# A third tile for the pre-mix's input in a talking-heads attention and MoE kernel

## The chip, the cores and the metric

The kernel runs on one core of one Trainium2 chip. The metric is device time in microseconds (us) of one execution, as the median of several runs; lower is better. TensorE multiplies matrices, VectorE (DVE) and ScalarE (ACT) work on elements, GpSimd (POOL) does a few elementwise steps, and SyncE (SP) issues DMAs. ScalarE and GpSimd can issue DMAs too.

## What is computed

Attention with 4 batches, 12 heads, 448 tokens and 64 dimensions, in which the scores of the 12 heads are mixed before the softmax (`w_pre`) and after it (`w_post`); then two feed-forward layers on the 1792 tokens.

```python
def _attn_ref(q, k, v, w_pre, w_post):
    scores = scale * np.matmul(q, k.transpose(0, 1, 3, 2))
    scores = np.einsum('bhij,hg->bgij', scores, w_pre)
    ...softmax over j...
    attn = np.einsum('bhij,hg->bgij', attn, w_post)
    return np.matmul(attn, v)
...
x = attn_out as (1792, 768)
x = elu(x @ moe_w_in) @ moe_w_out                     # 768 -> 2048 -> 768
x = layer_norm(solu(x @ moe2_w_in)) * g_ln @ moe2_w_out   # 768 -> 1024 -> 768
```

## The kernel before

**Chunks.** The attention runs over 17 chunks of query rows (`CH`), numbered 0 to 16. A chunk holds 4 to 12 groups of ten query rows of one batch. Chunks 0 to 4 belong to batch 0, 5 to 8 to batch 1, 9 to 12 to batch 2, 13 to 16 to batch 3.

**Scores and moves.** For each pair of heads of a chunk there is one score step on TensorE (`mm` in `add_score`, L443), which fills two PSUM banks. VectorE or ScalarE copies each bank to an SBUF buffer `sev` (`evac`, L449; 8 buffers, `SB`). A DMA, called a move here (`move`, issued at L400), then carries the rows of that head to their place in the chunk's tile `sp`, in which 12 heads of a group of query rows lie on neighbouring partitions. The last head takes two moves, so a chunk has 13. A `sev` buffer is free again when its move has landed.

**Pre-mix, softmax, post-mix.** Two groups make a unit; there are 90. A unit's pre-mix (`pre`, L510) multiplies the rows of `sp` with `wpre_t`. It needs all moves of the chunks that it reads, so the first unit of a chunk waits for the chunk's last move. VectorE finds the maximum (L515), ScalarE the exponential (L520), GpSimd the weights of the post-mix (L531), and TensorE does the post-mix (`post`, L543), whose result is copied to `at` (L551). When a chunk's units are through, TensorE multiplies `at` with the values (L592), and the result goes by way of `x` (L599) to `xs` in device memory.

**Two tiles.** `sp` has two tiles, in the pools `spa` and `spb`, that chunks use in turn: chunk c writes the tile of chunk c-2 (L453, L463). They are cleared once (L470), the first by VectorE, the other by GpSimd. The keys lie in a pool `k` of 12 tiles (L130); a batch needs six.

**What sets the order.** All steps of the attention are given to `op` with a rank (a planned time), what they depend on, the buffers that they take or use, and a cost on each engine that may do them. `schedule` (L296) then picks, again and again, the step that can start first and, on that engine, the one with the lowest rank, and emits it. So each engine's order is fixed when the program is built. The ranks of a chunk's scores are spread between the planned pre-mix start of the chunk ahead of it and `SCM` us ahead of its own (L391 to L393). With `lag` a step's result counts as there so many us after its planned end; moves have 3.5. The moves of chunks 0 and 1 may go by SP or ScalarE, those of chunk 2 by SP or GpSimd, all others by SP (L461).

**DMA completion.** The DMAs that SP and ScalarE issue share eight completion semaphores (`DMAHW0` to `DMAHW7` in the rows of order) by turns: each waits until the eighth before it in the program has landed. Those that GpSimd issues have others (`DMASW`).

After the attention, `start_moe` (L662) releases the pools on the right side of the memory and starts the loads of the first feed-forward layer.

Of the kernel before, what the change touches and what calls it, by code (L numbers as in the profile page):

```python
# [9 lines left out]
F32 = mybir.dt.float32  # L10
# [8 lines left out]
NB, NH, S, D = 4, 12, 448, 64  # L19
# [5 lines left out]
NC = len(CH)  # L25
# [12 lines left out]
XB = 2  # L38
# [12 lines left out]
DB = .9  # L51
DA = .2
T0 = 14
SCM = 12
KD = 3.5
VD = 28
WB = 3
SB = 8
VB = 2
EB = 10  # L60
LEAD = 3

@with_exitstack
def kernel(ctx: ExitStack, tc: tile.TileContext, qa, kt, vt, wpre, wpost,
# [6 lines left out]
    pools = {}  # L71

    def pool(name, bufs=1, side="left", space=None):
        kw = {"space": space} if space is not None else {"side": side}
        p = tc.alloc_tile_pool(name=name, bufs=bufs, reuse_waits="tile", **kw)
        pools[name] = p
        return p

    def release(*names):
        for n in names:  # L80
            pools.pop(n).release()
# [45 lines left out]
    wpost_t = const.tile([128, 60], F32, name="wpost_t")  # L127

    pool("spa", 1, "right")
    k_p = pool("k", 12, "right")  # L130
    kst_p = pool("kst", 2, "right")
    q_p = pool("q", 4, "right")
    sev_p = pool("sev", SB, "right")
# [72 lines left out]
    def w1_alloc(fg, p):  # L206
        w1[fg] = tuple(p.tile([128, 1536], F32R, tag=t, name=t) for t in ("wih", "wil", "woh", "wol"))
# [6 lines left out]
    def xT_alloc(tb, p):  # L214
        xT[tb] = (p.tile([128, ECH, S], F32R, name=f"xh{tb}"), p.tile([128, ECH, S], F32R, name=f"xl{tb}"))
# [63 lines left out]
    class Op:  # L279
# [2 lines left out]
    ops = []  # L282
    tail = {"pe": .3, "act": .2, "dve": .17, "pool": .1, "sp": 2.0, "host": 0.0}
    bufs = {"sc": 3, "pm": 3, "po": 2, "sev": SB, "e": EB, "wr": WB, "st": 4, "kst": 2, "q": 4,
            "k": 12, "sp0": 1, "sp1": 1, "at": 2, "v": VB, "x": XB, "ws": 4, "wy": 2}

    def op(rank, emit, deps=(), new=(), uses=(), more=0.0, lag=None, **us):

        o = Op()
        o.rank, o.emit, o.deps, o.new, o.us, o.more, o.lag = rank, emit, [d for d in deps if d is not None], new, us, more, lag  # L290
        for b in chain(new, uses):
            b.users.append(o)
        ops.append(o)
        return o
# [61 lines left out]
    def copier(e):  # L356
        return nc.scalar.copy if e == "act" else nc.vector.tensor_copy
# [6 lines left out]
    def plan_front():  # L364
        nonlocal t, nf
        if nf < NU:
            t_pre[nf] = t
            c = units[nf][1][0]
            t += PRE + (6 * SC / (first[c + 1] - first[c]) if c + 1 < NC else 0.0)
            nf += 1  # L370

    pending = []
    for u in range(NU):
        while nf < min(NU, u + LEAD + 1):
            plan_front()
# [14 lines left out]
    for c in range(NC):  # L390
        lo, hi = (t_pre[first[c - 1]], t_pre[first[c]] - SCM) if c > 1 else (T0 - 5, T0 - 1) if c else (2, T0 - 6)  # L391
        for h in range(0, NH, 2):
            t_sc[c, h] = lo + (h + 1) * (hi - lo) / NH  # L393

    kt_t, kb, q_t, qb_, sp_t, sp_op, pre_op, e_t = {}, {}, {}, {}, {}, {}, {}, {}
# [3 lines left out]
    def dma(out, in_, e="sp"):  # L399
        {"act": nc.scalar, "pool": nc.gpsimd, "sp": nc.sync}[e].dma_start(out=out, in_=in_)  # L400
# [27 lines left out]
    def add_score(c, h):  # L428

        b, _, G = CH[c]  # L430
        n = 5 * G
        ring = ("sc", "pm")[h // 2 % 2] if c == 0 else "sc"
        scb, svb = [Buf(ring) for _ in range(2)], [Buf("sev") for _ in range(2)]
        r = t_sc[c, h]
        key = "sc", c, h

        def mm(e):
            T[key] = [pools["ps_" + ring].tile([128, 512], F32, tag=ring, name="sc") for _ in range(2)]
            q, k = q_t[c, h // 6], kt_t[b, h]
            for x in range(2):  # L440
                for i in range(2):
                    sl = slice(64 * i, 64 * i + 64)
                    nc.tensor.matmul(T[key][i][64 * x:64 * x + 64, :S], q[sl, h % 6 // 2, 64 * x:64 * x + 64], k[sl, :],  # L443
                                     start=True, stop=True)

        def evac(e, i):
            t = T["sv", c, h + i] = (k0.tile([128, S], F32, name=f"s0_{h + i}") if c == 0 else
                                     sev_p.tile([128, S], F32, tag="sev", name="sev"))
            copier(e)(t, T[key][i][:, :S])  # L449

        def move(e, i, p, r0, r1):
            if c not in sp_t:
                sp_t[c] = sp_t[c - 2]  # L453
            dma(sp_t[c][p:p + 13 * (r1 - r0 - 1) + 1:13, 0:G, :], T["sv", c, h + i][r0 * G:r1 * G], e)

        o1 = op(r, mm, [k_op[b, h], q_op[c, h // 6]], scb, [qb_[c, h // 6], kb[b, h]], pe=SC)
        for i in range(2):
            sv = [] if c == 0 else [svb[i]]
            o2 = sc_ev[c, h + i] = op(r + .9 + .1 * i, lambda e, i=i: evac(e, i), [o1], sv, [scb[i]], act=.43, dve=.54)
            for n, to in enumerate([(h + i, 0, 10)] if h + i < 11 else [(11, 0, 5), (64, 5, 10)]):  # L460
                sp_op.setdefault(c, []).append(op(r + 2 + .2 * i + .1 * n, lambda e, i=i, to=to: move(e, i, *to), [o2], [spb_[c]], sv, lag=3.5, sp=.78, **({"act": .78} if c < 2 else {"pool": 1.0} if c == 2 else {})))  # L461

    spb_ = {c: Buf(f"sp{(NC - c) % 2}") for c in range(NC)}  # L463
    o = op(7.0, lambda e: dma(wpre_t, wpre), sp=.5)
    o_wpost = op(T0 + 2, lambda e: dma(wpost_t, wpost), sp=.5)
    w_op = op(T0 - 8, lambda e: nc.gpsimd.tensor_scalar(wpre_t, wpre_t, 0.125, None, ALU.mult), [o], pool=.6)

    for c in range(2):
        sp_t[c] = pools["spb" if (NC - c) % 2 else "spa"].tile([128, NH, S], F32, tag="sp", name="sp")
        (nc.gpsimd if c else nc.vector).memset(sp_t[c], 0.0)  # L470
    for t in po_p:
        nc.vector.memset(t, 0.0)
# [1 line left out]
    def begin(e):  # L474
        release("k0")
        pool("at", 2)
        pool("e", EB)
        pool("wr", WB)
# [4 lines left out]
    for c in range(NC):  # L483
        b = CH[c][0]
        if c == HEAD[b]:
            for h in range(0, NH, 2):
                add_k(b, h)
        for hf in range(2):
            add_q(c, hf)
        for h in range(0, NH, 2):  # L490
            add_score(c, h)
# [78 lines left out]
    for c in range(NC):  # L570
# [12 lines left out]
        for n in range(2):  # L583
            r = t_av[c, n]
# [76 lines left out]

    def start_moe(e):  # L662
        nonlocal gln_t
        release("sev", "q", "kst", "k", "spa")
        p = pool("wstg", 2, "right")
        gln_t = p.tile([128, F2 // 128], F32, name="gln_t", bufs=1)
        dma(gln_t, gln)
        w1_alloc(0, pool("w1a", 1, "right"))
        xT_alloc(0, pool("xT0", 1, "right"))

    gln_t = None
    lc = NC - 1
    t0 = t_pre[first[lc]]
    o_moe = op(t0, start_moe, sp_op[lc] + [pre_op[last_of[lc - 1]], T["ws", 15]] +
               [k_op[NB - 1, NH - 2]], host=0.0)
    need = []
# [41 lines left out]
    for i in range(3):  # L718
        ws = Buf("ws")
# [252 lines left out]
```

## Time and profile before

| | us |
|---|---|
| median of 3 runs | 1096.0 (1095.16 to 1097.95) |
| the profiled execution, its own time | 1094.9 |
| its span, first to last instruction | 1093.1 |
| TensorE busy in the span | 1059.9 (97%) |
| VectorE / ScalarE / GpSimd busy | 722.0 / 504.2 / 231.6 |

The attention takes the first 370 us or so; the first feed-forward layer runs up to about 840 us, the second to the end. In the list of the costliest groups the score, pre-mix and post-mix matmuls have 123.8, 112.2 and 109.1 us. A matmul's end is modelled, so two that follow closely are shown to overlap, and a short wait between them is not shown as idle time. A float32 matmul of the program stands as two records in the trace: a unit's pre-mix has four matmuls and eight records.

### The profile page before, as it was taken

What the parts mean: (1) busy time and instruction counts of PE and PEld (TensorE: products, weight loads), DVE (VectorE), ACT (ScalarE), POOL (GpSimd) and SP (SyncE); (2) the same over time, 40 slices, a digit from 0 to 9 for tenths busy, and PEclk for the clock granted to TensorE, in tenths of its full rate; (3) what the DMA queues carried; (4) which work ended last, traced back from release to release, by engine and by line L of the source; (5) the groups of instructions that cost most, each with busy time, mean ns of one, the idle gap of its engine ahead of it and who ended that gap; (6) DMA issues with size and microseconds to landing.
All of it is one profiled execution on the core that took longest, in us unless ns stands there. A gap on an engine that the chain in (4) does not pass through costs nothing.

```text
span 1093.1 us, 28427 instructions
## 1 busy us (share of the span) xinstructions
PE 1059.9 (97%) x11800; PEld 888.6 (81%) x11800; DVE 722.0 (66%) x1391; ACT 504.2 (46%) x1071; POOL 231.6 (21%) x243
## 2 busy tenths in 40 slices
PE   6899999999999999999999999999999999999998
PEld 2457667667666898998988999999999889898988
DVE  6576687677677557687887887878864644353522
ACT  3566676677676455333333443333431434342422
POOL 2211010011011325343343433343431000000000
PEclk9999999999999999999999999999999999999999
DMA  6875775775746442415234242423262400000001
GB/s 200 210 209 172 216 238 172 219 221 176 232 149 197 132 133 72 155 58 171 99 117 149 83 154 77 140 91 126 70 243 100 194 30 15 30 23 22 30 15 44
DMA packets 80287, 141.69 MB, mean 130 GB/s; under 512 B 20853, under 2 KB 59969, under 8 KB 80157
## 3 DMA queue, kind: packets, MB, share of 16 engines
q1 hardware_dynamic: 78345, 136.59, 39.1%
q10 hardware_dynamic: 1332, 2.09, 0.6%
q8 instruction: 93, 1.52, 0.6%
q0 software_dynamic: 480, 1.19, 0.4%
q14 instruction: 37, 0.30, 0.1%
HBM read 75.96 MB, written 25.17 MB: 93 GB/s over the span
## 4 chain that ended last, share of the span: by engine, by line
PE 74%; DMA 9%; DVE 8%; ACT 4%; issue 2%; SPq 1%; POOL 1%; ACTq 0%; DVEq 0%; POOLq 0%
PE h L256 15%; PE o L745 15%; PE o L888 11%; PE h L841 11%; PE av L592 6%; PE sc L443 5%; PE pm L510 5%; PE po L543 5%; DMA sp<-sev 3%; DMA ws<-in_wo_dram 2%; DVE x L761 1%; DVE wy L184 1%; DMA ws<-in_wi_dram 1%; PE tr L872 1%; DVE wq L180 1%
## 5 line engine op out<-in xcount | busy, mean ns | idle before, releaser
L520 ACT ACTIVATE e<-pm,st 128x448 f32<-128x448 f32 x180 | 113.4, 635 | 72.3 <-DVE st L515 65.9
L515 DVE TENSOR_REDUCE st<-pm 128x1 f32<-128x448 f32 x180 | 105.1, 617 | 60.9 <-PE pm L510 58.6
L745 PE MATMUL o<-gh,woh 128*128 128x448 f32 x384 | 141.3, 368 | 3.8 <-ACT x L759 1.9
L745 PE MATMUL o<-glo,woh 128*128 128x448 f32 x384 | 139.9, 364 | 0.0
L745 PE MATMUL o<-gh,wol 128*128 128x448 f32 x384 | 139.8, 364 | 0.0
L443 PE MATMUL sc<-kt,q 64*64 64x448 f32 x816 | 123.8, 565 | 9.7 <-ACT sev L449 4.6
L543 PEld LDWEIGHTS po<-wr,e 60*64 60x64 f32 x5040 | 102.4, 135 | 37.0 <-issue 23.8
L269 POOL TENSOR_TENSOR glo<-g,gh 128x448 fp32r<-128x448 f32 x64 | 83.1, 1298 | 217.9 <-issue 124.5
L510 PE MATMUL pm<-sp,wpre_t 64*64 64x448 f32 x720 | 112.2, 558 | 10.4 <-DMA xs<-x 4.4
L888 PE MATMUL o<-w,lh 128*128 128x384 f32 x448 | 120.3, 340 | 0.0
L543 PE MATMUL po<-wr,e 60*64 60x60 f32 x5040 | 109.1, 219 | 2.3 <-issue 1.1
L841 PE MATMUL h<-w,x2h 128*128 128x512 f32 x336 | 107.7, 395 | 0.0
L761 DVE TENSOR_TENSOR x<-x,o 128x448 f32<-128x448 f32 x168 | 101.4, 610 | 7.9 <-PE o L745 7.9
L256 PE MATMUL h<-xh,wih 128*128 128x448 f32 x288 | 105.5, 366 | 0.0
L256 PE MATMUL h<-xh,wil 128*128 128x448 f32 x288 | 105.0, 365 | 0.0
L256 PE MATMUL h<-xl,wih 128*128 128x448 f32 x288 | 104.9, 364 | 0.0
L264 ACT ACTIVATE t<-t 128x448 f32<-128x448 f32 x64 | 37.0, 578 | 134.7 <-DVE t L263 134.7
L531 POOL TENSOR_TENSOR wr<-wpost_t,st 128x120 f32<-128x120 f32 x90 | 36.3, 403 | 294.7 <-DVE st L527 225.7
L592 PEld LDWEIGHTS av<-at,v 128*64 128x64 f32 x1632 | 75.8, 137 | 14.1 <-DVE st L515 3.5
L592 PE MATMUL av<-at,v 128*64 128x120 f32 (+5 forms) x1632 | 83.2, 258 | 3.3 <-issue 1.8
L745 PEld LDWEIGHTS o<-gh,woh 128*128 128x128 f32 x384 | 72.1, 188 | 12.7 <-DVE x L761 4.5
L888 PEld LDWEIGHTS o<-w,lh 128*128 128x128 f32 x448 | 81.7, 188 | 0.6
(98 smaller groups left out, 1930.2 us busy)
## 6 DMA issues: line engine op xcount, KB each, us to landing
sp<-sev SPq DMA_DIRECT2D x94, 210.0 KB
ws<-in_wi_dram SPq DMA_DIRECT2D x33, 512.0 KB
ws<-in_wo_dram SPq DMA_DIRECT2D x21, 512.0 KB
q<-in_qa_dram SPq DMA_DIRECT2D x34, 192.0 KB
v<-in_vt_dram SPq DMA_DIRECT2D x24, 256.0 KB
w2s<-ws SPq DMA_DIRECT2D x12, 512.0 KB
ws<-in_wo_dram SPq DMA_DIRECT2D x16, 384.0 KB
w2s<-ws SPq DMA_DIRECT2D x16, 384.0 KB
```

Of the source, the lines that this page charges most:

```text
L256: nc.tensor.matmul(ps[:, :S], a[:, kc * FG + ft * 128:kc * FG + (ft + 1) * 128], x[:, kc, :], start=kc == 0 and n == 0, stop=kc == ECH - 1 ...
L269: nc.gpsimd.tensor_tensor(glo, g, f(gh), ALU.subtract)
L443: nc.tensor.matmul(T[key][i][64 * x:64 * x + 64, :S], q[sl, h % 6 // 2, 64 * x:64 * x + 64], k[sl, :], start=True, stop=True)
L510: nc.tensor.matmul(ps_t[u][r][64 * s:64 * s + 64, :S], wpre_t[p, :], sp_t[c][p, g, :], start=True, stop=True)
L515: nc.vector.tensor_reduce(out=st_t[u][:P, r:r + 1], in_=ps_t[u][r][:P, :S], op=ALU.max, axis=AX.X, negate=True)
L520: nc.scalar.activation(out=t[:P], in_=ps_t[u][r][:P, :S], func=AF.Exp, bias=st[:P, r:r + 1], scale=1.0, accum_out=st[:P, 2 + r:3 + r])
L543: nc.tensor.matmul(out[:, :, 5 * r:5 * r + 5], e_t[u, r][sl, 64 * n:64 * n + 64], wr_t[u][sl, r].rearrange("p (g a) -> p g a", a=5), start ...
L592: nc.tensor.matmul(ps[64 * k:64 * k + 64, i, :], v_t[CH[c][0]][:, 6 * n + 2 * i + k, q, :], at_t[c][:, q, 6 * n + 2 * i + k, :w], start=q ...
L745: nc.tensor.matmul(ps[:, :S], a[:, ft * DM + e * 128:ft * DM + (e + 1) * 128], x, start=n == 0, stop=n == 5)
L761: nc.vector.tensor_tensor(x1[tb][:, e, :], x1[tb][:, e, :], ps[:, :S], ALU.add)
L841: nc.tensor.matmul(ps[:, hf * 512:hf * 512 + 512], a[:, k, :], w, start=n == 0, stop=n == 3 * ECH - 1)
L888: nc.tensor.matmul(ps[:, :384], a[:, k, :], w, start=n == 0, stop=n == 3 * FC - 1)
```

## The change

- `sp` gets a third tile, in a new pool `spc`; chunk c writes the tile of chunk c-3. The third is cleared by GpSimd as well.
- To make room, the pool of keys has 8 tiles in place of 12.
- `SCM` goes from 12 to 18.
- The planned `lag` of a move is 5.0 in place of 3.5 from chunk 2 on.
- The moves of chunk 2 may go by SP or ScalarE; none goes by GpSimd.

```diff
-SCM = 12
+SCM = 18
...
+KB = 8
...
     pool("spa", 1, "right")
-    k_p = pool("k", 12, "right")
+    pool("spc", 1, "right")
+    k_p = pool("k", KB, "right")
...
-            "k": 12, "sp0": 1, "sp1": 1, "at": 2, "v": VB, "x": XB, "ws": 4, "wy": 2}
+            "k": KB, "sp0": 1, "sp1": 1, "sp2": 1, "at": 2, "v": VB, "x": XB, "ws": 4, "wy": 2}
...
-                sp_t[c] = sp_t[c - 2]
+                sp_t[c] = sp_t[c - 3]
...
-                sp_op.setdefault(c, []).append(op(..., lag=3.5, sp=.78, **({"act": .78} if c < 2 else {"pool": 1.0} if c == 2 else {})))
+                sp_op.setdefault(c, []).append(op(..., lag=3.5 if c < 2 else 5.0, sp=.78, **({"act": .78} if c < 3 else {})))
...
-    spb_ = {c: Buf(f"sp{(NC - c) % 2}") for c in range(NC)}
+    spb_ = {c: Buf(f"sp{(NC - c) % 3}") for c in range(NC)}
...
-    for c in range(2):
-        sp_t[c] = pools["spb" if (NC - c) % 2 else "spa"].tile([128, NH, S], F32, tag="sp", name="sp")
+    for c in range(3):
+        sp_t[c] = pools["spa spb spc".split()[(NC - c) % 3]].tile([128, NH, S], F32, tag="sp", name="sp")
         (nc.gpsimd if c else nc.vector).memset(sp_t[c], 0.0)
...
-        release("sev", "q", "kst", "k", "spa")
+        release("sev", "q", "kst", "k", "spc", "spa")
```

The order of instructions follows from the planner, so it shifts everywhere in the attention. Line numbers rise by 2 behind the new lines (L449 becomes L451, L400 becomes L402).

**ScalarE, while the moves of chunk 2 are issued.** A row of 10x12x448 is a move of chunk 2, `sev<-sc` is a copy of a score bank, `e<-pm` an exponential of chunk 1's first units. Before:

```order
L449 COPY sev_405<-sc_391 128x448 [waits DMAHW7_49,PE_49]
L551 COPY at_398<-po0_119 128x48x10 [waits DMAHW3_49,DMAHW4_49,DVE_49,PE_49]
L449 COPY sev_450<-sc_440 128x448 [waits DMAHW1_49,PE_49]
L449 COPY sev_469<-sc_454 128x448 [waits DMAHW6_49,PE_49]
L520 ACTIVATE e_485,st_482<-pm_463,st_482 128x448 [waits DVE_49]
L449 COPY sev_487<-sc_475 128x448 [waits DMAHW0_49,PE_49]
L520 ACTIVATE e_497,st_482<-pm_464,st_482 128x448 [waits DVE_49]
```

and now:

```order
L451 COPY sev_412<-sc_398 128x448 [waits DMAHW7_49,PE_49]
L402 DMA sp_137<-sev_412 10x12x448 [waits DMAHW5_49,Activation_49,Pool_49]
L402 DMA sp_137<-sev_414 5x12x448 [waits DMAHW7_49,DVE_49]
L451 COPY sev_455<-sc_446 128x448 [waits DMAHW1_49,PE_49]
L451 COPY sev_458<-sc_447 128x448 [waits PE_49]
L402 DMA sp_137<-sev_458 10x12x448 [waits DMAHW2_49,Activation_49]
L451 COPY sev_474<-sc_460 128x448 [waits PE_49]
L402 DMA sp_137<-sev_474 10x12x448 [waits DMAHW4_49,Activation_49]
L522 ACTIVATE e_490,st_486<-pm_468,st_486 128x448 [waits DVE_49]
L451 COPY sev_492<-sc_480 128x448 [waits DMAHW0_49,PE_49]
L402 DMA sp_137<-sev_492 10x12x448 [waits DMAHW6_49,Activation_49]
L522 ACTIVATE e_510,st_486<-pm_469,st_486 128x448 [waits DVE_49]
```

Moves stand between the copies and exponentials, each with a wait for a DMA semaphore; the copy to `at` went to VectorE.

**SP, at the first moves of chunk 3.** `kst` is a load of weights for the next layer, `xs<-x` a store of chunk 0's result, `q` a load of queries; the 10x12x448 rows from `kst` on are moves of chunk 3. Before:

```order
L400 DMA kst<-in_wi_dram 128x192
L400 DMA xs_59<-x 128x3x40
L400 DMA sp<-sev 10x12x448 x4
L400 DMA xs_59<-x 128x3x40
L400 DMA q<-in_qa_dram 128x384
L400 DMA sp<-sev 10x12x448 x2
L400 DMA q<-in_qa_dram 128x384
L400 DMA sp<-sev 10x12x448 x2
```

and now:

```order
L402 DMA kst<-in_wi_dram 128x192
L402 DMA sp<-sev 10x12x448 x2
L402 DMA xs_59<-x 128x3x40 x2
L402 DMA sp<-sev 10x12x448 x2
L402 DMA q<-in_qa_dram 128x384
L402 DMA sp<-sev 10x12x448 x2
L402 DMA q<-in_qa_dram 128x384
L402 DMA sp<-sev 10x12x448 x2
```

The first two moves of chunk 3 stand ahead of chunk 0's stores now.

**SP, from chunk 13 to chunk 14.** Moves of chunk 13 are 10x11x448, those of chunk 14 10x12x448; `v` is a load of values. Before:

```order
L400 DMA sp<-sev 10x11x448 x3
L400 DMA w1s_92<-kst 128x192
L400 DMA sp<-sev 10x11x448 x3
L400 DMA kst<-in_wo_dram 128x192
L400 DMA sp<-sev 10x11x448 x2
L400 DMA v<-in_vt_dram 128x512
L400 DMA q<-in_qa_dram 128x384
L400 DMA v<-in_vt_dram 128x512
L400 DMA sp<-sev 10x11x448 x2
L400 DMA q<-in_qa_dram 128x384
L400 DMA xs_61<-x 128x3x120
```

and now:

```order
L402 DMA sp<-sev 10x11x448 x7
L402 DMA w1s_92<-kst 128x192
L402 DMA sp<-sev 10x11x448
L402 DMA kst<-in_wo_dram 128x192
L402 DMA sp<-sev 10x11x448 x2
L402 DMA v<-in_vt_dram 128x512
L402 DMA q<-in_qa_dram 128x384
L402 DMA sp<-sev 10x12x448 x2
L402 DMA q<-in_qa_dram 128x384
L402 DMA xs_61<-x 128x3x120
```

Chunk 13's last two moves no longer stand behind loads of values, and chunk 14's first two stand ahead of the store.

## Rows read from the trace of the kernel before

**Rows 1.** Stretches: us, busy us by engine (instructions), TensorE's clock, DMA share, GB/s.

```profile
60.00:350.00 290.00, 277.69 (x6885) 193.97 (x6881) 210.21 (x529) 194.66 (x521) 31.66 (x79) 1.00 0.67 200
600.00:1093.00 493.00, 489.44 (x2480) 447.70 (x2478) 290.41 (x499) 176.61 (x294) 89.87 (x72) 1.00 0.23 82
```

**Rows 2.** Waits of TensorE: line, releaser, us in total, times, longest.

```profile
PE pm L510 <- DMA xs<-x: 4.4, 3, 1.9
PE pm L510 <- DMA sp<-sev: 4.1, 5, 1.3
```

**Rows 3.** Timeline of TensorE: start, us, line, records [idle before, releaser].

```profile
17.85 1.29 PE L510 MATMUL pm<-sp,wpre_t 64*64 64x448 f32 x8
...
50.74 0.98 PE L510 MATMUL pm<-sp,wpre_t 64*64 64x448 f32 x8 [0.82 <-DMA sp<-sev]
...
71.60 0.93 PE L510 MATMUL pm<-sp,wpre_t 64*64 64x448 f32 x2 [1.93 <-DMA xs<-x]
73.03 0.60 PE L510 MATMUL pm<-sp,wpre_t 64*64 64x448 f32 x3 [0.50 <-DMA sp<-sev]
...
73.43 0.58 PE L510 MATMUL pm<-sp,wpre_t 64*64 64x448 f32 x3
...
90.69 0.94 PE L443 MATMUL sc<-kt,q 64*64 64x448 f32 x8
91.45 1.11 PE L510 MATMUL pm<-sp,wpre_t 64*64 64x448 f32 x5
...
133.81 1.00 PE L510 MATMUL pm<-sp,wpre_t 64*64 64x448 f32 x5 [1.34 <-DMA xs<-x]
...
218.42 1.57 PE L510 MATMUL pm<-sp,wpre_t 64*64 64x448 f32 x5
...
219.79 0.58 PE L510 MATMUL pm<-sp,wpre_t 64*64 64x448 f32 x3
...
240.35 1.20 PE L510 MATMUL pm<-sp,wpre_t 64*64 64x448 f32 x5 [0.54 <-DMA sp<-sev]
...
278.17 0.97 PE L510 MATMUL pm<-sp,wpre_t 64*64 64x448 f32 x4
280.26 0.59 PE L510 MATMUL pm<-sp,wpre_t 64*64 64x448 f32 x2 [1.12 <-DMA xs<-x]
...
280.66 0.57 PE L510 MATMUL pm<-sp,wpre_t 64*64 64x448 f32 x2
...
301.33 1.11 PE L510 MATMUL pm<-sp,wpre_t 64*64 64x448 f32 x5 [1.09 <-DMA q<-in_qa_dram]
```

**Rows 4.** Chain that ended last, pieces at moves: start, us, what.

```profile
41.14 9.36 DMA sp<-sev
...
65.41 7.49 DMA sp<-sev
...
230.96 9.26 DMA sp<-sev
```

**Rows 5.** Instructions on tile sp: count, ns least/median/most, first and last start.

```profile
L400 SPq DMA_DIRECT2D sp<-sev x194: 721/756/1861, 18.9 to 335.8; - x194
...
L400 ACTq DMA_DIRECT2D sp<-sev x8: 784/786/800, 15.1 to 26.5; - x8
L400 POOL DMA_DIRECT2D sp<-sev x6: 582/584/780, 27.8 to 42.3; - x6
...
L470 POOL MEMSET sp<- x1: 4578/4578/4578, 0.7 to 0.7; 128x5376 f32 x1
...
DMA to landing us min/median/max: 7.2/8.1/9.5
```

**Rows 6.** Timeline of ScalarE, at chunk 1's first exponential.

```profile
36.08 0.64 ACT L520 ACTIVATE e<-pm,st 128x448 f32<-128x448 f32 x1 [4.93 <-DVE st L515]
```

**Rows 7.** One stretch of 5 us, columns as in rows 1.

```profile
40.00:45.00 5.00, 5.00 (x178) 4.01 (x176) 3.21 (x7) 3.70 (x11) 1.62 (x3) 1.00 0.92 232
```

**Rows 8.** Waits of SP's queue, columns as in rows 2.

```profile
SPq L400 <- PE sc L443: 8.6, 7, 2.5
```

More of the change, by code (lines that the diff above doesn't have):

```diff
@@ L460, in add_score @@
             for n, to in enumerate([(h + i, 0, 10)] if h + i < 11 else [(11, 0, 5), (64, 5, 10)]):
-                sp_op.setdefault(c, []).append(op(r + 2 + .2 * i + .1 * n, lambda e, i=i, to=to: move(e, i, *to), [o2], [spb_[c]], sv, lag=3.5, sp=.78, **({"act": .78} if c < 2 else {"pool": 1.0} if c == 2 else {})))
-    spb_ = {c: Buf(f"sp{(NC - c) % 2}") for c in range(NC)}
+                sp_op.setdefault(c, []).append(op(r + 2 + .2 * i + .1 * n, lambda e, i=i, to=to: move(e, i, *to), [o2], [spb_[c]], sv, lag=3.5 if c < 2 else 5.0, sp=.78, **({"act": .78} if c < 3 else {})))
+    spb_ = {c: Buf(f"sp{(NC - c) % 3}") for c in range(NC)}
     o = op(7.0, lambda e: dma(wpre_t, wpre), sp=.5)
```

## The prediction

> **What bounds the kernel now.** I read the stretches first, then TensorE's waits, then its rows at the places where a chunk begins, then the chain. Between 60 and 350 us, the attention part, TensorE is busy for 277.69 of 290 us, VectorE for 210.21 and ScalarE for 194.66; from 600 us on TensorE is busy for 489.44 of 493 [rows 1]. So TensorE sets the time, the expert layers leave nothing to gain, and what a change of the attention part can win is idle TensorE time there.
>
> Of that idle time the list of waits puts 4.4 us on `xs<-x` and 4.1 on `sp<-sev`, all of it before a pre-mix matmul (L510) [rows 2]; 1.09 more, before chunk 14, is put on `q<-in_qa_dram` [rows 3]. The pre-mix reads only `sp` and the small weight `wpre_t`, and DMAs of all kinds take turns on eight semaphores, so the name can be that of another DMA on the same one. I take all 9.6 us as waits for score moves, since the place fits: each falls on the first pre-mix unit of a chunk.
>
> The rows of TensorE show those starts [rows 3]. A unit is eight matmul records and takes about 0.98 us where nothing holds it. Chunk 2 waits at 50.74 (0.82), chunk 3 at 71.60 and 73.03 (1.93 and 0.50), chunk 6 at 133.81 (1.34), chunk 11 at 240.35 (0.54), chunk 13 at 280.26 (1.12), chunk 14 at 301.33 (1.09). Idle time as shown is too little: a matmul's shown end covers part of a stall. Chunk 3's first unit runs from 71.60 to 74.01, 2.41 us; take off 0.98 and the 0.50 shown, and 0.93 is hidden. Chunk 13's runs from 278.17 to 281.23: 3.06 less 0.98 and 1.12 leaves 0.96. Chunk 10's runs from 218.42 to 220.37 with no idle shown: 0.97 hidden. Chunk 4, at 91.45, shows no idle before it.
>
> The chain says the same: it goes through moves that were issued at 41.14, 65.41 and 230.96 and took 9.36, 7.49 and 9.26 us to land [rows 4]. The first ends at 50.50, just ahead of chunk 2's start at 50.74, the second at 72.90, just ahead of 73.03. A move is late because its score was late, by a few us out of a chunk of about 21.
>
> **The change, part by part.** *Third tile and SCM.* The constant moves the rank of a chunk's scores from 12 to 18 us ahead of its pre-mix, and the third tile lets a move of chunk c be issued before the pre-mix of chunk c-2 is through. In the order of TensorE I counted the work that lies between a chunk's last score and its first pre-mix unit. A score step counts 0.76 us, as from 90.69 to 91.45 [rows 3]; for the others I used the planner's own numbers (pre-mix 0.76, post-mix 0.83, attention times values 2.6). The cover grows for most chunks after the second: chunk 3 from 7.0 to 9.6 us, 6 from 8.9 to 11.7, 10 from 8.4 to 12.1, 11 from 11.5 to 12.3, 13 from 7.5 to 9.9, 14 from 6.6 to 9.3. It shrinks for chunk 5 (7.6 to 7.3) and chunk 7 (13.4 to 11.8), and neither waited. The missing time at the chunks that wait, idle and hidden, is 3.4 us at chunk 3, 2.1 at 13 and about 1 at the others, so added cover of 2.4 us or more removes nearly all of it, except at chunk 11, whose late landing comes from a 9.26 us flight.
>
> The gain at chunks 3 to 16 is then the shown idle, 1.93 + 0.50 + 1.34 + 0.54 + 1.12 + 1.09 = 6.5 us, and the hidden part, 0.93 + 0.96 + 0.97 = 2.9 us: 9.4 us [rows 3]. The shown part alone, 6.5, is the lower end if the hidden part is only modelled ends. What remains of it? TensorE is in order and the post-mix trails three units behind, so a stall at a chunk's start delays all that follows; but VectorE is at 72% and ScalarE at 67% [rows 1], and a TensorE that arrives sooner will now and then wait for a copy or an exponential. I leave a quarter for that: 9.4 x 0.75 = 7.0 us gained. The bounds are 0 (all of it turns into other waits) and 9.4.
>
> *Chunk 2's moves from GpSimd to ScalarE.* Six issues leave GpSimd, where one took 584 ns, and six come to ScalarE at 786 ns each [rows 5], 6 x 0.786 = 4.7 us of an engine that also copies scores and does the exponentials. Queued behind each is the next copy or exponential, and TensorE waits for those through the PSUM banks. They fall between 28 and 45 us, where ScalarE is idle for 4.93 us at one stretch [rows 6], enough to hide the issue time if all of it fell there. But the moves on SP and ScalarE also share the eight semaphores: each waits until the eighth DMA before it has landed, and ScalarE stands still for that time; the moves on GpSimd had others. Moves by GpSimd took 7.2 to 9.5 us to land [rows 5]. Following ScalarE's new order row by row, I find it late by one issue (0.8 us) when it comes to the exponentials of the second unit of chunk 1, and chunk 2's last score, which now stands behind one more pre-mix unit, later by about as much again. Lower end: -1.0 us (chunk 2's 0.82 and the rest of its wait vanish); upper end: all six issues on the path, 4.7 us. I take a loss of 1.2, between those 0.8 and 1.6, nearer to what the idle of [rows 6] leaves than to the full price.
>
> On this point the rows first: moves issued by GpSimd (7.2 to 9.5 us) and one issued by SP (9.36 us) at the same time landed equally late [rows 4, 5], with the DMA engines busy for 0.92 of the time between 40 and 45 us [rows 7]. The Trainium skill (DMA: Bandwidth & Descriptors, section Issuing engines are not separate DMA queues) says that DMAs from any engine run on the same 16 DMA engines and that issuing from several saves only the time to issue. By that rule the trace agrees, and chunk 2 would gain nothing in landing; by the opposite, six free queues, it would gain its 0.82 us.
>
> *Third memset.* GpSimd clears one more tile, 4578 ns [rows 5], right behind the first, so until about 10 us (twice 4.6 and a start within the first us). Next on GpSimd is the scaling of the pre-mix weight, which the first pre-mix needs at 17.85 us [rows 3]: hidden, with over 7 us to spare; without that cover it would cost 4.6 us.
>
> *k in 8 tiles in place of 12.* A batch needs six. Four of the six loads for the next batch now wait until the old batch's last scores have read their tile, on SP, in front of the moves. SP's waits for score matmuls are 8.6 us in 7 cases now, 2.5 at most [rows 8]. The loads are a chunk ahead of their use, so TensorE sees nothing; if one holds SP, it costs up to 2.5 us at each of three batch changes, 7.5 at most. I take 0.
>
> *The rest.* The planned landing time of a move goes from 3.5 to 5.0 us, which only orders instructions. Copies are shifted between VectorE and ScalarE by a few; their number is the same.
>
> Sum: the profiled execution took 1094.9 us (span 1093.1). 1094.9 - 7.0 + 1.2 = 1089.1. The median of the runs is 1096.0, 1.1 above the profiled one, so I forecast 1090.2, rounded to 1090.
>
> **Rivals.** *The stalls only change their name (no difference).* TensorE arrives sooner at the chunk's start and waits instead for VectorE's maximum or ScalarE's exponential, or SP cannot issue sooner: a move takes it 756 ns [rows 5], 13 moves 9.8 us of a 21 us chunk, and it holds them behind stores that wait for a copy. For it: both elementwise engines are near 70% [rows 1]. Against it: chunk 4, with 10.7 us of cover in the order before, starts at 91.45 without a wait [rows 3]. Then a quarter of 9.4 stays: -2.4 + 1.2, which gives 1094.8. The same time comes if the change does not do what it says, because SP's order puts the moves no earlier; in the order of SP the moves of chunks 3 and 14 do come sooner.
>
> *ScalarE blocks in the front (slower).* If each of its six issues waits for a landing, up to the 9 us of flight less the time since the eighth DMA before, ScalarE is late by more than its idle time. At 2.5 us each it is 6 x (0.8 + 2.5) = 20 us of ScalarE, less 4.9 idle [rows 6], so 15 us for the exponentials of chunk 1 and the scores of chunk 2; the gain at later chunks stays 7.0, which gives 1096.0 - 7.0 + 15 = 1104. It takes all the gain where 6 x (0.8 + w) - 4.9 = 7.0, that is from a wait w of 1.2 us per issue on. For it: flights of 7 to 9.5 us there [rows 4, 5]. Against it: eight DMAs issued at about one per us by two engines are themselves some 8 us of program, so most have landed when their turn comes.
>
> **How the numbers follow.** Within 0.3%, 3.3 us, a measurement of this kernel can't tell a difference. The forecast's gain of 5.8 has 0.58: faster. No difference 0.27, slower 0.15. The range goes from full removal with no loss in the front, 1096.0 - 9.4 - 1.0 = 1085.6, and 1 us of spread, to 1098.0: past the no-difference case, 1094.8, by 3 us for a front up to its full 4.7, and short of most of the slower case.
>
> **What would show it.** In the profile after, the waits of the pre-mix for DMAs should fall from 9.6 us to 3 or less, with chunk 1's and 2's left; TensorE busy between 60 and 350 us should be a greater share; chunk 2's start should be within 1.5 us of 50.74, and ScalarE should show no gap over 2 us before a move between 28 and 45 us. The forecast is wrong if chunk 2 starts past 55 us, or if the waits before L510 go and those before the score and post-mix matmuls grow by as much.

## The result, and the profile after

The changed kernel takes 1085.56 us (median of 5 runs, 1085.06 to 1086.96); the kernel before, measured beside it, 1095.16 (5 runs, 1091.4 to 1097.95). The ratio is 0.9915, 95% interval 0.9891 to 0.9939: 9.6 us gained, where 5.8 were forecast. The profiled execution took 1086.96 us, with a span of 1085.2; the one of before took 1094.9 with 1093.1. So the two traces differ by 7.9 us, and they can be cut at the same work: at the first pre-mix of chunk 2, at that of chunk 16, and at the first output matmul of the feed-forward (L745 before, L747 after). First before, then after; the columns are those of [rows 1].

```profile
0.00:50.74 50.74, 37.96 (x585) 17.66 (x585) 29.52 (x54) 21.80 (x50) 11.24 (x18) 0.97 0.72 205
50.74:341.55 290.81, 279.64 (x6944) 196.75 (x6945) 210.11 (x531) 194.15 (x519) 30.39 (x78) 1.00 0.66 197
341.55:383.28 41.73, 39.92 (x754) 31.89 (x753) 27.51 (x50) 23.80 (x54) 14.32 (x13) 1.00 0.56 171
383.28:1093.10 709.82, 702.33 (x3521) 642.26 (x3519) 454.81 (x757) 264.44 (x448) 175.70 (x135) 1.00 0.27 94
```

```profile
0.00:49.42 49.42, 37.57 (x592) 17.48 (x593) 30.65 (x56) 21.14 (x50) 11.99 (x13) 1.00 0.70 211
49.42:330.47 281.05, 274.40 (x6937) 195.51 (x6937) 207.89 (x532) 196.29 (x524) 30.28 (x78) 1.00 0.70 205
330.47:375.57 45.10, 40.51 (x752) 33.10 (x753) 31.02 (x49) 21.27 (x47) 18.24 (x14) 0.96 0.52 155
375.57:1085.20 709.63, 702.25 (x3521) 642.29 (x3519) 453.28 (x757) 264.25 (x448) 176.87 (x135) 1.00 0.27 94
```

The count of matmuls is the same in each part within 8, so the parts can be compared. The front gives 1.3 us. Chunks 2 to 16 give 9.8: 290.81 less 281.05. Of these, 4.5 are idle time (11.17 before, 6.65 after) and 5.2 are busy time, 279.64 less 274.40, seen most clearly in the group of the scores (before, then after: records, busy us, mean ns, idle time before them):

```profile
L443 PE MATMUL sc<-kt,q 64*64 64x448 f32 x656 | 95.8, 544 | 0.7 <-ACT sev L449 0.7
L445 PE MATMUL sc<-kt,q 64*64 64x448 f32 x648 | 90.5, 543 | 0.7 <-ACT at L553 0.7
```

The 8 records that are missing after are one score step, 0.76 us of work, which now stands ahead of chunk 2: at equal work the front gives about 2.1 us and the chunks 9.0. The other 4.5 us of busy time went for the same matmuls; I read them as time in which TensorE stood and the modelled ends covered it. Then 3.4 us are lost between chunk 16 and the first output matmul, 41.73 against 45.10, and the 710 us behind that are unchanged. 1.3 + 9.8 - 3.4 + 0.2 is the 7.9.

The waits of TensorE, which answer to [rows 2]: line, releaser, us in total, times, longest.

```profile
PE sc L445 <- ACT sev L451: 4.8, 4, 1.9
...
PE po L545 <- ACT at L553: 2.9, 2, 2.7
PE po L545 <- issue: 2.7, 5, 0.8
PE pm L512 <- ACT e L522: 2.3, 5, 0.7
...
PE pm L512 <- DMA sp<-sev: 0.4, 1, 0.4
```

The 4.4 us on `xs<-x`, the 4.1 on `sp<-sev` and the 1.1 on `q` before a pre-mix have become 0.4 in all. New are 2.9 us of the post-mix on ScalarE's copy L553, of which 2.7 in one wait: that one is in the tail, below. Taken together, the waits before the score and post-mix matmuls went from 11.6 to 16.4 us, 4.8 more, where those before the pre-mix for DMAs lost 9.2.

The starts of chunks 2, 3, 4, 6, 10, 11, 13, 14 and 16 in TensorE's timeline, as in [rows 3]:

```profile
49.42 0.98 PE L512 MATMUL pm<-sp,wpre_t 64*64 64x448 f32 x8 [0.40 <-DMA sp<-sev]
...
67.70 1.53 PE L512 MATMUL pm<-sp,wpre_t 64*64 64x448 f32 x5
69.03 0.58 PE L512 MATMUL pm<-sp,wpre_t 64*64 64x448 f32 x3
...
89.23 1.10 PE L512 MATMUL pm<-sp,wpre_t 64*64 64x448 f32 x8
...
126.94 1.02 PE L512 MATMUL pm<-sp,wpre_t 64*64 64x448 f32 x8
...
209.23 1.10 PE L512 MATMUL pm<-sp,wpre_t 64*64 64x448 f32 x8
...
230.08 1.10 PE L512 MATMUL pm<-sp,wpre_t 64*64 64x448 f32 x8
...
268.94 0.98 PE L512 MATMUL pm<-sp,wpre_t 64*64 64x448 f32 x8
...
289.95 1.21 PE L512 MATMUL pm<-sp,wpre_t 64*64 64x448 f32 x8
...
330.47 1.13 PE L512 MATMUL pm<-sp,wpre_t 64*64 64x448 f32 x8
```

Only chunk 2 shows idle time, and eight records take 0.98 to 1.21 us nearly everywhere. Chunk 3 still starts with a hidden stall: 67.70 to 69.61 is 1.91 us, 0.93 too long, where before it was 2.41 with 0.50 of it shown.

### The profile page after: what moved, and what is told of

Its sections match the earlier page's. It is cut to its first block, busy times and chain, and to the rows that moved or that the text cites. A ratio compares the mean times of both kernels' runs of the same rounds, so it can differ in the third digit from the quotient of the medians.

```text
span 1085.2 us, 28432 instructions
## 1 busy us (share of the span) xinstructions
PE 1054.7 (97%) x11800; PEld 888.4 (82%) x11800; DVE 722.9 (67%) x1393; ACT 502.9 (46%) x1068; POOL 237.4 (22%) x239
## 4 chain that ended last, share of the span: by engine, by line
PE 77%; DVE 8%; DMA 6%; ACT 3%; issue 3%; SPq 1%; POOL 1%; ACTq 0%; DVEq 0%; POOLq 0%
PE h L258 15%; PE o L747 15%; PE o L890 11%; PE h L843 11%; PE av L594 6%; PE po L545 6%; PE pm L512 6%; PE sc L445 6%; DMA sp<-sev 2%; DMA ws<-in_wo_dram 2%; DVE x L763 1%; DVE wy L186 1%; DMA ws<-in_wi_dram 1%; PE tr L874 1%; DVE wq L182 1%
## 5 line engine op out<-in xcount | busy, mean ns | idle before, releaser
L747 PE MATMUL o<-gh,woh 128*128 128x448 f32 x384 | 141.4, 368 | 3.8 <-ACT x L761 1.9
L517 DVE TENSOR_REDUCE st<-pm 128x1 f32<-128x448 f32 x180 | 105.7, 617 | 54.2 <-PE pm L512 52.3
L747 PE MATMUL o<-gh,wol 128*128 128x448 f32 x384 | 139.9, 364 | 0.0
L747 PE MATMUL o<-glo,woh 128*128 128x448 f32 x384 | 139.8, 364 | 0.0
L445 PE MATMUL sc<-kt,q 64*64 64x448 f32 x816 | 118.4, 558 | 10.6 <-ACT sev L451 4.8
L512 PE MATMUL pm<-sp,wpre_t 64*64 64x448 f32 x720 | 107.7, 554 | 4.7 <-ACT e L522 2.3
L258 PE MATMUL h<-xh,wih 128*128 128x448 f32 x288 | 105.8, 367 | 0.0
L258 PE MATMUL h<-xl,wih 128*128 128x448 f32 x288 | 105.2, 365 | 0.0
L258 PE MATMUL h<-xh,wil 128*128 128x448 f32 x288 | 105.0, 365 | 0.0
L533 POOL TENSOR_TENSOR wr<-wpost_t,st 128x120 f32<-128x120 f32 x88 | 34.2, 388 | 292.6 <-DVE st L529 240.5
L747 PEld LDWEIGHTS o<-gh,woh 128*128 128x128 f32 x384 | 72.0, 188 | 12.8 <-DVE x L763 4.5
```

Of the source, the lines that this page charges most:

```text
L258: nc.tensor.matmul(ps[:, :S], a[:, kc * FG + ft * 128:kc * FG + (ft + 1) * 128], x[:, kc, :], start=kc == 0 and n == 0, stop=kc == ECH - 1 ...
L512: nc.tensor.matmul(ps_t[u][r][64 * s:64 * s + 64, :S], wpre_t[p, :], sp_t[c][p, g, :], start=True, stop=True)
L517: nc.vector.tensor_reduce(out=st_t[u][:P, r:r + 1], in_=ps_t[u][r][:P, :S], op=ALU.max, axis=AX.X, negate=True)
L747: nc.tensor.matmul(ps[:, :S], a[:, ft * DM + e * 128:ft * DM + (e + 1) * 128], x, start=n == 0, stop=n == 5)
```

## Where the loss in the tail comes from

Rows of the changed kernel's timeline between chunk 16 and the first output matmul, engine by engine (start, us, engine, line, record, idle before and releaser):

```profile
344.51 1.70 DVE L225 CAST xh<-xst 128x896 fp32r<-128x896 f32 x1
346.13 2.05 DVE L526 TENSOR_SCALAR st<-st 128x2 f32<-128x2 f32 x1
348.10 1.08 DVE L230 TENSOR_TENSOR xl<-xst,xh 128x896 fp32r<-128x896 f32 x1
349.10 1.14 DVE L517 TENSOR_REDUCE st<-pm 128x1 f32<-128x448 f32 x2
...
351.64 0.17 DVE L526 TENSOR_SCALAR st<-st 128x2 f32<-128x2 f32 x1 [0.21 <-ACT e L522]
...
343.61 2.12 POOL L693 TENSOR_TENSOR wil<-wy,wih 128x512 fp32r<-128x512 f32 x1
345.78 2.38 POOL L230 TENSOR_TENSOR xT<-xst,xT 128x896 fp32r<-128x896 f32 x1
...
349.80 0.64 ACT L522 ACTIVATE e<-pm,st 128x448 f32<-128x448 f32 x1 [3.63 <-DVE st L517]
...
351.04 1.76 PE L545 MATMUL po<-wr,e 60*64 60x60 f32 x54 [2.69 <-ACT at L553]
352.73 0.74 PE L258 MATMUL h<-xh,wih 128*128 128x448 f32 x1
353.27 0.57 PE L258 MATMUL h<-xl,wih 128*128 128x448 f32 x1
```

Read it from below. TensorE stands for 2.69 us on ScalarE's copy; ScalarE stood for 3.63 on VectorE's maximum (L517); VectorE came to that late, because a step on two numbers per partition (L526) took 2.05 us. It takes 0.17 at 351.64. It ended at 348.18, when GpSimd's subtraction ended (345.78 + 2.38 = 348.16); the cast before it took 1.70 us, where the same cast took 0.62 at 339.97, and ended at 346.21, half a us behind the end of GpSimd's step before (345.73). That is 3 us late in all; a subtraction of VectorE's own (1.08 us) stands between the two-number step and the maximum as well. GpSimd is slow there too: its subtraction on 128x512 takes 2.12 us, and 1.27 at 336.19. Both prepare the feed-forward. Then TensorE's granted clock falls, and the first matmuls of L258 take 0.74 and 0.57 us where they take 0.36 later: TensorE had stood still just before. Two us of this part, columns as in [rows 1], at the lower of the clock's two levels, 1.2 GHz of 2.4:

```profile
351.00:353.00 2.00, 1.96 (x55) 1.85 (x56) 0.88 (x4) 1.11 (x4) 0.39 (x1) 0.50 0.21 37
```

The kernel before has the same hold in its tail, a two-number step of VectorE beside a subtraction of GpSimd:

```profile
355.70 2.06 DVE L524 TENSOR_SCALAR st<-st 128x2 f32<-128x2 f32 x1
355.45 2.27 POOL L228 TENSOR_TENSOR xl<-xst,xh 128x896 fp32r<-128x896 f32 x1
```

There TensorE has attention times values to do (2.68 us from 357.52) and shows no wait behind it. What differs is how the steps fall: five of GpSimd's preparation steps start in the 16 us behind chunk 16's first pre-mix in the changed kernel, two in the kernel before.

The Trainium skill (SBUF — State Buffer, section SBUF: two separate sides) says that VectorE and GpSimd share one pair of ports, which a VectorE step that runs in a two-port mode or has two inputs in SBUF contends for with a GpSimd step, and that whichever starts first holds it to its end while the other fully stands. Whether the two-number step ran in such a mode no row shows; its times agree: it starts behind GpSimd's subtraction and ends 0.02 us after it.

## The experiments

The kernels are told by their difference to the kernel before or to the changed one; ratios are to the kernel before in runs beside it.

**All moves of chunks 3 to 16 left out** (the kernel leaves out those copies; the rest runs as before):

```diff
-            dma(sp_t[c][...], T["sv", c, h + i][...], e)
+            if c < 3:
+                dma(sp_t[c][...], T["sv", c, h + i][...], e)
```

> The kernel before with its order unchanged, but the score moves of chunks 3 to 16 are not issued (182 of 221 DMAs); the pre-mix of those chunks reads what the first chunks left in the tiles. Theory (the waits at chunk starts are late moves, and TensorE has nothing else to wait for there): the idle time before the pre-mix at chunks 3 to 16 goes, 7 to 9 us less than before, about 1087 us. Rival (the stalls only change their name): under 3 us less, 1092 to 1096.

Measured 1081.18 us (0.9875, 0.9847 to 0.9904): 14 us less, where 7 to 9 were expected. This is what the moves cost in the kernel before, waits shown and hidden and whatever their traffic costs; the 9.4 us that the prediction read from the chunk starts is two thirds of it. TensorE is busy for 285.94 of the 290 us, with the DMA share halved:

```profile
60.00:350.00 290.00, 285.94 (x7194) 201.56 (x7188) 222.57 (x552) 204.38 (x543) 36.15 (x83) 0.99 0.33 94
```

**The third tile and the 8 k tiles alone**: the kernel before with these; SCM stays 12, the planned landing 3.5, chunk 2 by SP and GpSimd.

> Third tile and the smaller key pool alone: SCM 12, lag 3.5 and chunk 2's moves by SP or GpSimd as before. Theory (what helps is that scores stand earlier in TensorE's order; the tile by itself moves little): its order gives chunks 3, 6, 13 and 14 the same 7.0, 9.0, 7.5 and 6.6 us of cover as before, so within 3 us of before, 1092 to 1097. Rival (moves were held by the tile): at least 5 us less than before.

Measured 1091.22 us (0.9978, 0.9954 to 1.0002): no difference that can be told, though the interval leaves room for up to 5 us. Chunk 16 starts where it started before (341.8 us; before 341.55).

**Two tiles, the rest of the change kept**:

```diff
-                sp_t[c] = sp_t[c - 3]
+                sp_t[c] = sp_t[c - 2]
-    spb_ = {c: Buf(f"sp{(NC - c) % 3}") for c in range(NC)}
+    spb_ = {c: Buf(f"sp{(NC - c) % 2}") for c in range(NC)}
```

> The changed kernel with two tiles again (SCM 18, lag 5.0, 8 key tiles and ScalarE for chunk 2 stay). Theory (earlier scores): its cover at chunks 3, 6 and 14 is 9.6, 10.9 and 13.2 us, as after or more, but 8.1 at 13 and 7.4 at 16; most of the gain stays, 1086 to 1090. Rival (the tile is what lets moves go early): moves wait on SP for the pre-mix of chunk c-2 and the time is within 3 us of before, 1092 or more.

Measured 1083.38 us (0.9896, 0.9867 to 0.9925). Without the third tile the whole gain is there, more than was expected. The profile shows a score that waits 2.32 us for a load of queries:

```profile
145.20 0.98 PE L444 MATMUL sc<-kt,q 64*64 64x448 f32 x8 [2.32 <-DMA q<-in_qa_dram]
```

**Chunk 2's moves by SP and GpSimd again, the rest of the change kept**:

```diff
-lag=3.5 if c < 2 else 5.0, sp=.78, **({"act": .78} if c < 3 else {})
+lag=3.5 if c < 2 else 5.0, sp=.78, **({"act": .78} if c < 2 else {"pool": 1.0} if c == 2 else {})
```

> The changed kernel with chunk 2's moves by SP or GpSimd as before. My step (ScalarE's issues cost 1.2 us in the front): 1 to 2 us less than the changed kernel, chunk 2 starts a little earlier. Rival (ScalarE's issues hide, GpSimd's cost as much): within 1 us of it. If ScalarE blocked in the front: 4 us less or more.

Measured 1087.05 us (0.9922, 0.9893 to 0.9951), chunk 2 at 49.26 us where the changed kernel has 49.42. Who issues these six moves makes no difference that can be told. Its chunk 2:

```profile
49.26 1.65 PE L512 MATMUL pm<-sp,wpre_t 64*64 64x448 f32 x8 [1.94 <-DMA sp<-sev]
```

Here TensorE stands 1.94 us for the move, 0.40 in the changed kernel: without ScalarE's issues it comes sooner and waits longer, and the start comes out the same. That chunk 2 gains nothing in landing is also what the rule weighed in the prediction says (the Trainium skill, DMA: Bandwidth & Descriptors, Issuing engines are not separate DMA queues).

**The changed kernel once more**, beside the next three:

> The changed kernel itself, beside the three below on one chip, so that they compare with it directly. Both theories: as measured first, about 1085.6 us, 0.9915 of the kernel before.

Measured 1084.91 us (0.9900, 0.9870 to 0.9931).

**SCM 18 alone**:

```diff
-SCM = 12
+SCM = 18
```

> The kernel before with SCM 18 alone: two tiles, 12 key tiles, lag 3.5, chunk 2 by SP or GpSimd. Theory (earlier scores are the gain, since the run without the third tile was at 0.9896 of before): cover of 8.8, 11.7, 11.7 us at chunks 3, 6 and 14 but 7.3 at 12, 6.5 at 13; 6 to 11 us less than before, 1084 to 1089. Rival (lag 5.0 is what spaces the moves): under 4 us less.

Measured 1084.4 us (0.9899, 0.9870 to 0.9928): this one number gives all that the change gives. With two tiles it still waits at a chunk start (3.2 us for `sp<-sev` in one wait before L510, at chunk 2), but it loses nothing in the tail. Its part from chunk 16 to the first output matmul:

```profile
332.23:371.80 39.57, 37.97 (x697) 30.52 (x697) 27.16 (x49) 21.38 (x50) 18.16 (x16) 1.00 0.55 171
```

This part has 697 matmuls, not 752, because the post-mix of one more unit, about 1 us, stands ahead of chunk 16 there; it idles for 1.6 us, the changed kernel's for 4.6. By the first output matmul (371.82 us) it is 3.75 us ahead of the changed kernel (375.57), in these two profiles; the medians, 1084.4 and 1084.91, differ by 0.5.

**The two subtractions of the feed-forward's preparation on VectorE alone**, in the changed kernel:

```diff
-        return op(r + 5, lo, [o], [], [wy], pool=1.25, dve=.6)
+        return op(r + 5, lo, [o], [], [wy], dve=.6)
-        return op(r + 5, lambda e: x_lo(tb, i, eng[e]), [o2], [], [ws], pool=2.1, dve=1.0)
+        return op(r + 5, lambda e: x_lo(tb, i, eng[e]), [o2], [], [ws], dve=1.0)
```

> The changed kernel, but the differences (xl, wil, wol) that prepare the feed-forward layer while the last units of the attention run go to VectorE alone, not to GpSimd. Theory (in the last 20 us VectorE stands still while GpSimd reads and writes SBUF: a maximum came 3 us late, and TensorE waited 2.69 us): VectorE's small steps fall from 2 us to 0.2, TensorE's wait of 2.69 us goes, from chunk 16's first unit to the first output matmul 45.1 us become 40 to 42, 3 to 5 us less in all. Rival (VectorE is late since it has too much to do there): no better or slower, as it gets 5 us more work.

Measured 1079.68 us (0.9850, 0.9817 to 0.9883), 5.2 us under the changed kernel beside it. Its VectorE at the same place, then its part from chunk 16 to the first output matmul:

```profile
344.72 1.27 DVE L230 TENSOR_TENSOR xT<-xst,xT 128x896 fp32r<-128x896 f32 x1
345.92 0.41 DVE L690 CAST woh<-wy 128x512 fp32r<-128x512 f32 x1
346.25 0.16 DVE L526 TENSOR_SCALAR st<-st 128x2 f32<-128x2 f32 x1
```

```profile
327.49:369.20 41.71, 39.51 (x754) 32.16 (x754) 26.77 (x51) 22.57 (x50) 7.49 (x9) 1.00 0.55 169
```

VectorE has more to do, 1.27 us for what took GpSimd 2.38, and the two-number step takes 0.16 us. The part is back at 41.71 us, as before the change, the clock at 1.00, and the 2.69 us wait is gone. So the cause of the loss in the tail is shown: without these steps on GpSimd it is gone. That they held VectorE is read from the rows above.

**The feed-forward's preparation starts later** (it waits for a pre-mix unit of the last chunk):

```diff
-    o_moe = op(t0, start_moe, sp_op[lc] + [pre_op[last_of[lc - 1]], T["ws", 15]] +
+    o_moe = op(t0, start_moe, sp_op[lc] + [pre_op[first[lc] + 1], T["ws", 15]] +
```

> The changed kernel, but the start of the feed-forward layer's preparation waits for the second unit of chunk 16. Theory (the third tile let this preparation start sooner, into the last softmax units, and that lost 3.4 us of the 11.1 us gained): the stretch from chunk 16's first unit to the first output matmul goes from 45.1 to about 41 us, 2 to 4 us less in all. Rival (the first hidden matmul then waits for its operands): equal or slower.

Measured 1082.81 us (0.9882, 0.9852 to 0.9912). Chunk 16 to the first output matmul takes 44.0 us there: with the steps still on GpSimd, a later start gives back about 1 of the 3.4 us. GpSimd's rows do not bear out the premise that the preparation starts sooner: its first step there stands 5.7 us behind chunk 16's first pre-mix in the changed kernel, 5.0 before.

**The same edit in the kernel before**, and in the kernel with SCM 18 alone:

> The kernel before, with the two subtractions of the feed-forward's preparation (add_w's lo, add_x's lo) on VectorE alone. Theory (the 3.4 us that the changed kernel loses between chunk 16's first pre-mix and the first output matmul come from VectorE standing while GpSimd runs these steps, and the kernel before, with 41.7 us there, loses little in the same way): 1092 to 1095 us, at most 2 us under the kernel before. Rival (the edit is worth the same in any kernel, 5 us): 1089 to 1090 us.

> The kernel before with SCM 18 alone (two tiles, chunk 2's moves by SyncE and GpSimd), and with the same two subtractions on VectorE alone. Theory (the third tile's 2 to 3 us in the chunks are real and show once the tail is no longer held): SCM 18 alone had 39.6 us in the tail already, so the edit gives at most 1 us, 1083.5 to 1084.5 us, 4 to 5 us above the changed kernel with the edit. Rival (the third tile is worth nothing at all): the same time as the changed kernel with the edit, within 1.5 us, near 1080 us.

Measured 1095.53 us (1.0006, 0.9979 to 1.0033) and 1084.4 us (0.9896, 0.9863 to 0.9929). Neither gains that can be told: in the kernel before, GpSimd's hold of VectorE (2.06 us, above) did not fall on a step that the end waits for. Of the three, the edit is worth something only in the changed kernel.

**The changed kernel with that edit again, and with SCM 24**:

> The changed kernel with the two subtractions on VectorE alone, once more. Theory: 1079 to 1081 us, 5 us under the changed kernel. Rival (the 5 us were that chip's or that run's): 1083 to 1086 us.

> The same kernel with SCM 24 in place of 18: in the order, the matmul work between a chunk's last score and its first pre-mix unit then is 13 to 19 us in nearly every chunk, where the changed kernel has 7 to 12. Theory (with SCM 18 the last move of a chunk lands 0.3 to 6.5 us ahead of its first pre-mix, so nothing is left to be had from an earlier landing): 1078 to 1081 us. Rival (the landing still holds the chunks, in waits that carry other names): 2 to 4 us less again, 1075 to 1077 us.

Again: 1078.31 us (0.9859, 0.9822 to 0.9896), the best of all, 17 us under the kernel before. Against SCM 18 alone with the same edit it is 6.1 us less (two runs of the one, 0.9850 and 0.9859; of two tiles with and without the edit, 0.9896 and 0.9899). With the tail mended these medians say that the third tile, with what comes with it, is worth some 4 to 6 us; the intervals overlap, so it is likely and not shown. Nor is it shown that the changed kernel gains this in the chunks and loses it in the tail: in two profiles its chunk 16 starts at 330.47 and 331.57 us, with SCM 18 alone at 332.23, where about 1 us more of work was done.

SCM 24 was a miss: 1087.72 us (0.9929, 0.9906 to 0.9952), 9 us more. Its TensorE in the front and later, then its stretch from 15 to 60 us:

```profile
34.94 5.76 PE L445 MATMUL sc<-kt,q 64*64 64x448 f32 x24 [4.98 <-DMA q<-in_qa_dram]
42.09 0.98 PE L512 MATMUL pm<-sp,wpre_t 64*64 64x448 f32 x8 [1.38 <-DMA sp<-sev]
...
136.59 0.98 PE L445 MATMUL sc<-kt,q 64*64 64x448 f32 x8 [1.44 <-DMA q<-in_qa_dram]
...
288.99 1.34 PE L545 MATMUL po<-wr,e 60*64 60x60 f32 x41 [3.08 <-issue]
```

```profile
15.00:60.00 45.00, 36.12 (x666) 18.56 (x668) 25.07 (x56) 21.11 (x55) 2.71 (x7) 0.92 0.74 212
```

Scores that stand further ahead meet a q that has not landed: 4.98 and 1.44 us, and in the part that holds the first of these the clock is 0.92. That is a bound which the prediction did not look at. In the changed kernel no score shows such a wait; with SCM 18 and two tiles one did, 2.32 us (above). These waits are 7.8 us with the 1.38; the 3.08 at 288.99, for nothing that the profile shows, stays open.

## Why the prediction was right, and where it was not

**The bound, and where the gain lies: right.** TensorE set the time, the idle time sat at the chunks' starts, and the waits before the pre-mix went from 9.6 us to 0.4, where 3 or less was asked. TensorE's share between 60 and 350 us rose from 277.69 to 280.35 of 290, although that stretch now holds the tail's beginning. Chunk 2 starts 1.3 us from 50.74. The waits before score and post-mix matmuls grew by 4.8 us, half of what went before the pre-mix and not as much, which was the sign of a wrong forecast; 2.7 of it is the tail's.

**The term of the chunks, -7.0: too small; it measured -9.8.** It is 9.0 at equal work. Two steps failed. The hidden part was read only at three starts, 2.9 us, while the busy time shrank by some 4.5 for the same matmuls; in the order of before, the kernel without moves puts the whole at 14. And the quarter kept back for VectorE and ScalarE does not show under their names: between chunks 2 and 16 TensorE's waits for them fell from 2.4 to 0.9 us, and of the 2.9 us on `at` 2.7 lie in the tail. What did grow there is idle time for nothing that the profile shows, from 2.0 to 5.5 us; the 9.8 are net of it, and what it waits for stays open.

**The credit to the third tile: wrong.** The prediction counted cover in the new order and did not part the constant from the tile. The runs do: SCM 18 alone 0.9899, the tile alone 0.9978. The cover that mattered was had with two tiles.

**ScalarE's six issues, +1.2: wrong; nothing.** The whole front became 1.3 us shorter, and with SP and GpSimd as issuers chunk 2 starts within 0.2 us of the same time. TensorE does come later to chunk 2 with ScalarE as issuer, as its shorter wait there shows (0.40 us against 1.94); what the term left out is that TensorE would else have stood for the move. Here is ScalarE at its moves:

```profile
27.46 0.53 ACT L451 COPY sev<-sc 128x448 f32<-128x448 f32 x1 [2.34 <-DMA sp<-sev]
28.57 1.66 ACTq L402 DMA_DIRECT2D sp<-sev  x2
30.33 0.97 ACT L451 COPY sev<-sc 128x448 f32<-128x448 f32 x2 [2.33 <-DMA q<-in_qa_dram]
```

It does stand, for 2.34 and 2.33 us, 1.66 of the second being two issues. The condition that ScalarE show no gap over 2 us was thus not met, and yet nothing came of it: the gaps replace idle time that it had anyway [rows 6]. The slower rival rested on such gaps at every issue; there are two.

**Third memset and k tiles, 0: right as far as seen.** GpSimd clears two tiles by about 10 us:

```profile
L472 POOL MEMSET sp<- x2: 4578/4578/4579, 0.7 to 5.2; 128x5376 f32 x2
```

The first pre-mix starts at 17.6 us, at 17.85 before, and no wait for a `kt` load appears but the one at the start that was there before. The tile-alone kernel, which has both, is no slower.

**Not in the prediction: the tail.** A new wait did take the place of some of those removed, but no rival named this place or VectorE and GpSimd as its cause. That the time fell into the range, which began at 1085.6 less 1 us, is in part luck: without the 3.4 us lost in the tail it would have been below it, as the kernel with the subtractions moved is (1079.68). On the profiled executions the forecast's 5.8 us became 7.9: 2.8 more in the chunks, 2.5 in the front (1.3 gained in place of 1.2 lost), 3.4 less in the tail, 0.2 elsewhere. From the 1096.0 that the forecast started from, the median is 10.4 us away, 2.5 more than between the profiles, since the profile of after is 1.4 above its median and that of before was 1.1 below the one it was set against.

**What stays open.** With the two subtractions moved, the order up to chunk 16 is the same as in the changed kernel on every engine, yet chunk 16 starts at 327.49 and 325.97 us in two profiles, against 330.47 and 331.57 in two of the changed kernel. The subtractions are not what brings it forward: with the later start, where they are still on GpSimd, it stands at 327.18:

```profile
327.18 1.10 PE L512 MATMUL pm<-sp,wpre_t 64*64 64x448 f32 x8
```

So executions of one order differ by 5 us and more there, and the tail accounts for 3.4 of the 5 to 6 us between the two kernels; where the rest comes from was not settled. Nor was the third tile tried alone with SCM 18 and everything else as before.

## What to carry to other kernels

Where a transfer lands late at a stage's start, move its producer ahead first and see whether the buffers already allow it; another buffer is a second step, and here it was worth nothing that could be told without the first. How far ahead is bounded by the producer's own inputs: past that, it waits for its load, as the scores did here for 4.98 us. And when a stage starts sooner, look at what overlaps at its end: a preparation that was harmless can fall beside the last work that the end waits for.

## What the runs showed of the hardware

A VectorE step of 0.17 us took 2.05 beside a GpSimd subtraction of 2.38, with the same end; GpSimd's own small step (L533, 0.39 us) took up to 1.06 in the kernel where VectorE does those subtractions. TensorE's granted clock was 0.50 in the 2 us after a single wait of 2.69, which makes 0.96 of the part of 45 us around it, and 0.92 in one of 45 us that held waits of 4.98 and 1.38. In 656 and 648 score matmuls the mean duration shown stayed at 544 and 543 ns while the busy time fell from 95.8 to 90.5 us, of which 0.8 is the missing step: the mean of one record shows nothing of a stall that the union of the records does.
